# Attention scores as half-height matmuls on two halves of the array rows, and second-MoE slots of 288 rows

## The chip, the core and the metric

One core of a Trainium2 chip runs the whole program in one launch. The metric is the device time of one execution in microseconds (us). TensorE (PE, with its weight loads shown apart as PEld), VectorE (DVE), ScalarE (ACT), GpSimd (POOL) and the DMA queues work side by side and wait for each other through semaphores.

## The reference, cut to what matters

```python
# attention: 4 batches, 8 heads, 576 tokens, head size 64
scores = q @ k.T / 8
scores = where(scores >= max(scores) - tau, scores, -1e9)
x = softmax(scores) @ v                  # then heads joined: 2304 x 512
# first MoE: 512 -> 2048 -> 512
x = square(relu(x @ w_in)) @ w_out
# second MoE: 8 experts, 512 -> 1024 -> 512, each token to one expert
e = argmax(x @ w_gate)
out = gate_w * eom * (relu(x @ w1[e]) @ w2[e])
```

## The kernel before

All large products are float32r matmuls in three terms: each operand is split into a part that the array takes exactly (`[.., 0, ..]`, made on ACT) and the rest (`[.., 1, ..]`, made on DVE), and high*high, high*low and low*high are added in PSUM. A planner (`Graph.schedule`) sets the order of every engine's instructions from estimated durations and keys; the order is then fixed, and each engine works through its own list.

**Attention** (from 6 us to about 430 us). Two heads share a pair (16 pairs); a pair's q and k lie with one head in partitions 0 to 63 and the other in 64 to 127. A chunk (`t_chunk`, 144 of them) is 128 queries against 576 keys: scores (L636), row maximum on DVE (L639), exponential on ACT (L642), threshold on POOL, mask and sum on DVE (L651), scaling on POOL (L662), five transposes on PE (L705), copies on ACT (L713); `t_av` multiplies with v (L733) in matmuls that fill 64 array columns each, two side by side. The contraction of one head is only 64 long. So `t_op` builds, for each head, a 128-row operand by SBUF-to-SBUF DMA (`opA`, `opB`): k's high part above its low part, and q turned to match. Two 128-row steps then give all four products. Each step is two matmuls of 288 keys (`hf`), so a chunk has 4 matmuls. Eight of nine steps in `STEPS` are such chunks; the ninth (`hd == 2`) takes the last 64 queries of both heads with a block-diagonal q (`xd`) in three 128-row steps, 6 matmuls. The first four chunks (`EARLY`, L672) read q and k in place, in 64 array rows: the first two in rows 0 to 63, the next two in rows 64 to 127.

**First MoE.** The hidden layer (`t_h`, L843, matmuls of 288 columns) is woven into the attention as soon as a batch is done; the output layer follows (`t_y`, L1004, 256 columns). After each 256 tokens `t_gate` picks the experts.

**Second MoE** (from 687 us). Tokens of an expert are gathered by an indirect DMA into slots (`t_slot`): 256 rows ("p", `U == 2`: 96 matmuls of 256 columns, L1301, then 48 of 512, L1351) or 128 rows ("s": 24 of 512, L1321, and 24 of 512, L1351). Every slot loads its expert's two weight matrices. Two slots of 256 are filled early; `t_table` on DVE computes from the counts which expert the other 7 and 4 slots hold (`S2`, `S1`). More slots would run in a branch (`extra`). The counts of this input are 110, 394, 153, 77, 281, 410, 499 and 380 tokens; the 13 slots hold them without the branch.

Of the kernel before, what the change touches and what calls it, by code (L numbers as in the profile page):

```python
# [261 lines left out]
def moa(ctx, tc, q, k, v, tau, w_in, w_out, wg, wog, w1, w2, ctab, coln, out):  # L262
# [35 lines left out]
    W1, W2 = 55, 8.0  # L298
# [6 lines left out]
    W4 = 30  # L305
    W6 = 197
    W7 = 130
# [3 lines left out]
    S2 = 7  # L311
    S1 = 4
    NL2, NL1 = 12, 8
# [16 lines left out]
        "scores": (-6, -3),  # L330
        "max": (-17, 14),
        "exp": (17, 2),
        "bound": (-27, -12),
        "mask": (-19, -32),
        "sum": (-16, -6),
        "norm": (-19, 35),
        "turn": (8, 11),
        "parts": (8, 9),
        "av": (4, -17),
        "prep": (-2, 13),  # L340
        "x": (8, 22),
# [15 lines left out]
    MEMF, MEMR = 10608, 25728  # L357
# [78 lines left out]
    for nm, n, shape in (  # L436
        ("xk", 2, [P, 2, S]), ("xq", 1, [P, 2, S]), ("xd", 1, [P, 2, P]),
        ("opA", 2, [P, OPN]), ("opB", 2, [P, OPN]),
    ):
        at = mk(nm, at, n, shape, F32R)  # L440
# [9 lines left out]
    at = mk("gs", at, 2, [P, 256], F32, 2)  # L450
# [4 lines left out]
    at = mk("lt", at, 3, [P, 2, 2], I32, 2)  # L455
    at = mk("cs", at, 3, [P, 2], F32, 2)
    at = mk("tb", at, 1, [P, 576], F32, 2)
    at = max(at, DEC)
# [5 lines left out]
    mk("xg", at, 1, [P, 2, DM + 1], F32, 3)  # L464
# [3 lines left out]
    at = mk("raw", at, 1, [P, 2, 512], F32, 3)  # L468
    mk("wgb", 0, 1, [P, NKC, 32], F32R, 2)
# [5 lines left out]
    at = mk("w", ATT, 4, [P, 2, 512], F32R, 2)  # L475
    at = mk("x2", at, 2, [P, 2, NKC, 256], F32R, 2)
    mk("w", at, 1, [P, 2, 512], F32R, 2)
    mk("hT", OPS, 2, [P, 2, DFE // P, 256], F32R, 3)
# [17 lines left out]
    tabn = const.tile([P, 3], I32, name="tabn")  # L496
# [86 lines left out]
    def t_op(pr, j, key):  # L583

        xk, xq = xks[pr], xqs[pr]
        buf = opb[pr, j] = new("opB" if j else "opA", f"{pr}")
        rows = slice(64 * j, 64 * j + 64)
        q3 = lambda r: buf.t[r, S:].rearrange("p (x n) -> p x n", x=2).bitcast(F32)

        def put_k(x):  # L590
            nc.sync.dma_start(buf.t[64 * x : 64 * x + 64, :S].bitcast(F32), xk.t[rows, x].bitcast(F32))

        def put_q():
            nc.sync.dma_start(q3(slice(0, 64)), xq.t[rows, :, 64:].bitcast(F32))

        def turn_q(x):
            nc.sync.dma_start(q3(slice(64, 128))[:, 1 - x], xq.t[rows, x, 64:].bitcast(F32))

        parts = lambda xy, *xs: [t for x in xs for t in (q_tags(pr, x) if xy is xq else [(xy, x)])]
        for x in range(2):  # L600
            dma(lambda x=x: put_k(x), 64 * S * 4, parts(xk, x), [(buf, "k", x)], key)
        dma(put_q, 64 * 1024 * 4, parts(xq, 0, 1), [(buf, "q")], key)
        for x in range(2):
            dma(lambda x=x: turn_q(x), 64 * 512 * 4, parts(xq, x), [(buf, "t", x)], key)
# [10 lines left out]
    def t_chunk(n, key):  # L615
# [6 lines left out]
        halves = [slice(hf * HALF, (hf + 1) * HALF) for hf in range(2)]  # L622
        q0 = QOFF[c]
        xk = xks[pr]

        def mm():
            if hd == 2:

                xd = xds[pr].t
                ops = [(xd[:, x], xk.t[:, y]) for x, y in ((0, 0), (0, 1), (1, 0))]  # L630
            else:
                o = opb[pr, hd].t
                ops = [(o[:, S + i * 512 + q0 : S + i * 512 + q0 + P], o[:, :S]) for i in range(2)]
            for i, (qo, ko) in enumerate(ops):
                for hf in range(2):
                    nc.tensor.matmul(s.t[:, hf, :HALF], qo, ko[:, halves[hf]], start=(i == 0), stop=(i == len(ops) - 1))  # L636
# [27 lines left out]
        if n < EARLY:  # L664
            xq = xqs[pr]
            hr = slice(64 * hd, 64 * hd + 64)

            def mm():
                i = 0
                for qx, kx in ((0, 0), (0, 1), (1, 0), (1, 1)):  # L670
                    for hf in range(2):
                        nc.tensor.matmul(  # L672
                            s.t[:, hf, :HALF], xq.t[hr, qx, 64 + q0 : 64 + q0 + P], xk.t[hr, kx, halves[hf]],
                            start=(i == 0), stop=(i == 3),
                        )
                    i += 1

            rd = [(xk, x) for x in range(2)] + [(xq, x, 0) for x in range(2)]
            g.add("PE", c_pe(HALF) * 8, mm, rd, [s], key)
        elif hd == 2:  # L680
            rd = [(xk, x) for x in range(2)] + [(xds[pr], j) for j in range(2)]
            g.add("PE", c_pe(HALF) * 6, mm, rd, [s], key + K("scores", pr))
        else:
            o = opb[pr, hd]
            rd = [(o, "q")] + [(o, w, x) for w in "kt" for x in range(2)]
            g.add("PE", c_pe(HALF) * 4, mm, rd, [s], key + K("scores", pr))
# [270 lines left out]
    turn = {"op": []}  # L957
# [87 lines left out]
    def t_gate(v, key):  # L1045
        row = rows[v]
        x2 = Buf(ALL["x2"], f"yT{v}")
# [18 lines left out]
        def mm():  # L1066
            for kc in range(NKC):
                for x in range(2):
                    nc.tensor.matmul(lt.t[:32], wgb.t[:, kc], x2.t[:, x, kc],
# [77 lines left out]
    def t_transpose(src, i, x2, tag, key, rd, G=g, pool=ALL):  # L1147
# [4 lines left out]
        def tp():  # L1152
            for kc in range(NKC):
                nc.tensor.transpose(ps.t[:, kc * P : (kc + 1) * P], src.t[:, i, kc * P : (kc + 1) * P], ident)

        dst = lambda x: x2.t[:, x, :, i * P : (i + 1) * P]
        p3 = lambda: ps.t.rearrange("p (c n) -> p c n", c=NKC)
        grp("PE", 0.45, tp, rd, [ps], key)
        grp("ACT", c_act(512, True), lambda: nc.scalar.activation(dst(0), p3(), AF.Copy), [ps], [(x2, 0, i)], key)
        grp("DVE", c_dve(512), lambda: nc.vector.tensor_tensor(dst(1), p3(), dst(0).bitcast(F32), op=ALU.subtract),  # L1160
# [4 lines left out]
    def t_table(early, key):  # L1165

        tt, ts, stt = nc.vector.tensor_tensor, nc.vector.tensor_scalar, nc.vector.scalar_tensor_tensor
        def run():
# [3 lines left out]
            Q = view(tb.t[:, 72:88], [P, 2, 8], F32)  # L1172
            sq = view(tb.t[:, 96:160], [P, 8, 8], F32)

            def cum(n):
                tt(sq, n.rearrange("p (o e) -> p o e", o=1).broadcast_to([P, 8, 8]), ct("le", [P, 8, 8]), op=ALU.mult)
# [21 lines left out]
            if early:  # L1198
                nc.vector.tensor_copy(t, cnt)
                ts(full, t, 8, None, op0=ALU.arith_shift_right)  # L1200
                cum(full)
# [5 lines left out]
            ts(t, cnt, 127.0, None, op0=ALU.add)  # L1207
            ts(t, t, 7, None, op0=ALU.arith_shift_right)
            stt(t, d, -2.0, t, op0=ALU.mult, op1=ALU.add)
            ts(a, t, 1, None, op0=ALU.arith_shift_right)  # L1210
# [11 lines left out]

            ts(tmp[:, 0:1], tabn[:, 0:1], float(S2), None, op0=ALU.subtract)
            stt(tabn[:, 2:3], tabn[:, 1:2], float(S1), tmp[:, 0:1], op0=ALU.subtract, op1=ALU.max)
# [3 lines left out]
        grp("DVE", (2.73 if early else 5.89), run, [(c2, "base"), (c2, "tab")], [tb, "tabe" if early else "tabl"], key)  # L1228
# [3 lines left out]
    def t_slot(G, pool, tag, tab, s, U, rows_known, deps, key):  # L1232

        add = G.add
        n = U * P
# [4 lines left out]
        lt, xg, cs, x2, hT = (Buf(pool[x], f"{x}{tag}") for x in ("lt", "xg", "cs", "x2", "hT"))  # L1240
# [5 lines left out]
        def r_s():  # L1246
            regs["s"] = nc.sync.value_load(tab[0:1, s, 0:1], min_val=0, max_val=NLIST - 256)

        def f_list():
            nc.sync.dma_start(lt.t[:, :U], lst[bass.ds(regs["s"], n)].rearrange("(u p) t -> p u t", p=P))  # L1250
# [5 lines left out]
        for u in range(U):  # L1256
            add("POOL", 1.05,
                lambda u=u: nc.gpsimd.indirect_dma_start(
                    out=xg.t[:, u], out_offset=None, in_=y_scr[0:rows_known],
                    in_offset=bass.IndirectOffsetOnAxis(lt.t[:, u, 0:1].bitcast(U32), 0)),  # L1260
# [24 lines left out]
        for u in range(U):  # L1285
            t_transpose(xg, u, x2, f"x{tag}", key - 8, [(xg, u)], G, pool)
# [3 lines left out]
            [(xg, u) for u in range(U)] + [(x2, 0, u) for u in range(U)], [cs], key)  # L1290
        xr = [(x2, x, u) for x in range(2) for u in range(U)]
        combos = ((0, 0), (0, 1), (1, 0))
        if U == 2:
            for fc in range(8):
                ps = Buf(pool["ph"], f"h{tag}_{fc}")

                def mm(fc=fc, ps=ps):
                    i = 0
                    for a, x in ((0, 0), (1, 0), (0, 1)):
                        for kc in range(NKC):  # L1300
                            nc.tensor.matmul(ps.t[:, :256], w1b[kc][fc // 4].t[:, a, (fc % 4) * P : (fc % 4 + 1) * P],  # L1301
                                             x2.t[:, x, kc], start=(i == 0), stop=(i == 11))
                            i += 1

                add("PE", 12 * c_pe(256), mm, xr + [(w1b[kc][fc // 4], a) for kc in range(NKC) for a in range(2)], [ps],
                    key + 1.45 * fc)
                add("ACT", c_act(256, True),
                    lambda fc=fc, ps=ps: nc.scalar.activation(hT.t[:, 0, fc], ps.t[:, :256], AF.Relu),
                    [ps], [(hT, 0, fc)], key + 1.45 * fc)
                add("DVE", c_dve(256),  # L1310
                    lambda fc=fc, ps=ps: nc.vector.scalar_tensor_tensor(  # L1311
                        hT.t[:, 1, fc], ps.t[:, :256], 0.0, hT.t[:, 0, fc].bitcast(F32), op0=ALU.max, op1=ALU.subtract),
                    [ps, (hT, 0, fc)], [(hT, 1, fc)], key + 1.45 * fc)
        else:
            for h in range(2):
# [8 lines left out]
                for kc in range(NKC):  # L1324
                    add("PE", 3 * c_pe(512), lambda kc=kc, mm=mm: mm(kc), xr + [(w1b[kc][h], 0), (w1b[kc][h], 1)], [ps],
                        key + 2.6 * h + 0.65 * kc)
# [17 lines left out]
        k2 = key + (10.5 if U == 2 else 6.0)  # L1344
        for u in range(U):
# [8 lines left out]
            for fc in range(8):  # L1354
# [6 lines left out]
                [ps, cs], [ob], k2 + 5.2 * u + 5.2)  # L1361
# [7 lines left out]
    def pair_prep(pr, key):  # L1369
# [4 lines left out]
        for j in range(2):  # L1374
# [133 lines left out]
```

## Time and profile before

| what | value |
|---|---|
| median of 3 runs | 967.85 us (965.61 to 968.86) |
| the profiled execution | 965.47 us, span 963.7 us |
| PE busy | 932.3 us, 97% of the span |
| DVE, ACT, POOL busy | 716.4, 645.6, 361.3 us |
| granted TensorE clock | 0.998 |

PE's busy time includes the modelled tail of each matmul, so a pause shorter than that tail doesn't show as idle. The pace of a stream is read from the starts of rows that follow each other, not from the mean duration of one instruction.

### The profile page before, as it was taken

Reading aid. Unit: us, or ns where it says so; the run is one execution under the profiler, and the core shown is the slowest. Engines: PE = TensorE matmul, PEld = TensorE weight load, DVE = VectorE, ACT = ScalarE, POOL = GpSimd, SP = SyncE. Lnnn points to the kernel's source line nnn. Section 1 sums busy time; section 2 is a strip of 40 time slices with the busy share of each in tenths; the row PEclk is TensorE's granted clock in tenths of the full one; section 3 lists DMA queues with packets and bytes.
Section 4 is the critical chain, followed back from the end, with each engine's and each line's share of the span. In section 5 each row is a group of like instructions: output and inputs, shape, how many; then the busy total and the mean of one; then the engine's idle time right before and its main releaser. Section 6 shows DMA issues by size and latency. Waiting matters only on the chain. (4 is left out here: it accounts for less than half of the span.)

```text
span 963.7 us, 20604 instructions
## 1 busy us (share of the span) xinstructions
PE 932.3 (97%) x6842; PEld 846.0 (88%) x6842; DVE 716.4 (74%) x1635; ACT 645.6 (67%) x1431; POOL 361.3 (37%) x607
## 2 busy tenths in 40 slices
PE   7899999999999999999999999999898999999996
PEld 6667889889889889989999999999887989889895
DVE  6898988877777777788558767898778677777720
ACT  5898888878678777787554444444648676876731
POOL 4556778875656766642101000010113111211300
PEclk9999999999999999999999999999999999999999
DMA  6785797767778766478455888566959867977700
GB/s 176 181 221 141 204 253 201 213 166 212 234 214 231 228 198 201 158 226 246 136 143 133 190 185 194 134 171 140 260 170 338 307 229 262 309 248 257 264 23 25
DMA packets 162565, 193.25 MB, mean 201 GB/s; under 512 B 23567, under 2 KB 113167, under 8 KB 162450
## 3 DMA queue, kind: packets, MB, share of 16 engines
q1 hardware_dynamic: 158210, 181.33, 65.2%
q0 software_dynamic: 4096, 10.52, 3.5%
q8 instruction: 56, 0.92, 0.4%
q14 instruction: 59, 0.48, 0.2%
q10 hardware_dynamic: 144, 0.00, 0.0%
HBM read 122.39 MB, written 43.20 MB: 172 GB/s over the span
## 5 line engine op out<-in xcount | busy, mean ns | idle before, releaser
L651 DVE SCALAR_TENSOR_TENSOR memf<-banks,memf 128x576 f32<-128x576 f32 x144 | 116.3, 814 | 43.4 <-ACT memf L642 27.0
L843 PE MATMUL banks<-memr,w 128*128 128x288 f32 x960 | 145.0, 299 | 1.3 <-DVE memr L740 1.3
L843 PEld LDWEIGHTS banks<-memr,w 128*128 128x128 f32 x960 | 130.9, 188 | 5.3 <-issue 3.8
L1004 PE MATMUL banks<-w,memr 128*128 128x256 f32 x864 | 126.9, 284 | 0.0
L713 ACT ACTIVATE pt<-banks 128x384 f32<-128x384 f32 (+2 forms) x320 | 114.2, 419 | 14.0 <-PE banks L705 13.5
L642 ACT ACTIVATE memf<-banks,memf 128x576 f32<-128x576 f32 x144 | 107.1, 753 | 20.1 <-DVE memf L639 13.6
L984 ACT ACTIVATE memr<-memf 128x512 fp32r<-128x512 f32 x126 | 77.7, 631 | 63.3 <-PE banks L1004 57.4
L639 DVE TENSOR_REDUCE memf<-banks 128x1 f32<-128x576 f32 x144 | 107.5, 750 | 16.3 <-PE banks L636 14.6
L662 POOL TENSOR_SCALAR memf<-memf 128x576 f32<-128x576 f32 x136 | 112.9, 832 | 13.0 <-DVE memf L659 7.0
L636 PE MATMUL banks<-memr 128*128 128x288 f32 x592 | 108.8, 308 | 5.3 <-DVE memf L651 3.4
L1004 PEld LDWEIGHTS banks<-w,memr 128*128 128x128 f32 x864 | 112.3, 190 | 0.3
L705 PE MATMUL banks<-ident,memf 128*128 128x128 f32 x720 | 104.6, 274 | 6.3 <-ACT pt L713 4.2
L1004 PE MATMUL banks<-memr 128*128 128x256 f32 x648 | 99.6, 285 | 0.0
L705 PEld LDWEIGHTS banks<-ident,memf 128*128 128x128 f32 x720 | 84.2, 140 | 14.6 <-POOL memf L647 4.7
L880 POOL TENSOR_TENSOR memf<-memf 128x288 f32<-128x288 f32 x88 | 71.5, 822 | 66.4 <-DVE memf L880 37.0
L636 PEld LDWEIGHTS banks<-memr 128*128 128x128 f32 x592 | 83.8, 188 | 13.8 <-DVE memf L651 7.1
L1301 PE MATMUL banks<-memr,w 128*128 128x256 f32 x504 | 91.4, 283 | 0.9 <-DVE memr L1311 0.9
L1140 POOL DMA_INDIRECT lst<-memf x18 | 18.7, 1039 | 193.6 <-DVE memf L1132 108.8
L988 DVE TENSOR_TENSOR memr<-memf,memr 128x512 fp32r<-128x512 f32 x126 | 82.9, 695 | 10.5 <-ACT memr L984 10.5
L843 PE MATMUL banks<-memr 128*128 128x288 f32 x576 | 87.9, 299 | 0.9 <-ACT memf L849 0.9
L1004 PEld LDWEIGHTS banks<-memr 128*128 128x128 f32 x648 | 87.1, 190 | 0.0
L733 PE MATMUL banks<-pt,memf 128*64 128x256 f32 (+1 forms) x640 | 85.0, 411 | 1.2 <-DVE memf L651 0.9
(153 smaller groups left out, 1778.4 us busy)
## 6 DMA issues: line engine op xcount, KB each, us to landing
memf<-in_moe_w_dram SPq DMA_DIRECT2D x104, 512.0 KB
r_scr<-memf SPq DMA_DIRECT2D x192, 144.0 KB
memf<-r_scr SPq DMA_DIRECT2D x51, 512.0 KB
memr<-memr SPq DMA_DIRECT2D x64, 144.0 KB
memr<-memr SPq DMA_DIRECT2D x64, 128.0 KB
memr<-memr SPq DMA_DIRECT2D x32, 256.0 KB
memf<-in_moe_w_in_dram SPq DMA_DIRECT2D x32, 256.0 KB
memf<-in_moe_w_out_dram SPq DMA_DIRECT2D x32, 256.0 KB
```

The source lines that it names most:

```text
L636: nc.tensor.matmul(s.t[:, hf, :HALF], qo, ko[:, halves[hf]], start=(i == 0), stop=(i == len(ops) - 1))
L639: nc.vector.tensor_reduce(nm.t, s.t[:, :, :HALF], axis=AX.XY, op=ALU.max, negate=True)
L642: nc.scalar.activation(p.t[:, :S].rearrange("p (a n) -> p a n", a=2), s.t[:, :, :HALF], AF.Exp, bias=nm.t)
L651: nc.vector.scalar_tensor_tensor(p3, s.t[:, :, :HALF], th.t, p3, op0=ALU.is_ge, op1=ALU.mult, accum_out=sm.t)
L662: nc.gpsimd.tensor_scalar(p.t[:, :S], p.t[:, :S], sm.t, 1.0, op0=ALU.mult, op1=ALU.mult)
L705: nc.tensor.transpose(ps.t[:, i - a], p.t[:, i * P : (i + 1) * P], ident)
L713: lambda pt=pt, ps=ps, j=j, a=a, z=z, c0=c0, w=w, off=off: nc.scalar.activation(pt.t[:, j, a:z, off : off + w], ps.t[:, :, c0 : c0 + w], A ...
L733: nc.tensor.matmul(out(slice(64 * j, 64 * j + 64)), raw.t[:, j, c], pt.t[:, j, c, :N], start=(c == 0), stop=(c == NQ - 1))
L843: nc.tensor.matmul(ps.t[:, :HALF], wv[:, a, kc], xT.t[:, x, kc, half], start=(i == 0), stop=(i == len(seq) - 1),)
L988: lambda d=d, sq=sq: nc.vector.tensor_tensor(d(1), sq(), d(0).bitcast(F32), op=ALU.subtract),
L1004: nc.tensor.matmul(ps.t[:, :QT], o.t[:, a, f], w.t[:, x, cc], start=(f == 0 and i == 0), stop=(f == 7 and i == 2))
L1301: nc.tensor.matmul(ps.t[:, :256], w1b[kc][fc // 4].t[:, a, (fc % 4) * P : (fc % 4 + 1) * P], x2.t[:, x, kc], start=(i == 0), stop=(i == 11))
```

## The change

Scores: `t_op` now makes one tile for both heads (`ox`), in which each head's k and q lie in the other head's partitions; 4 DMAs a pair instead of 10. A chunk multiplies high*high, high*low and low*high in three steps (the fourth product is left out). In each step the first 288 keys are multiplied in array rows 0 to 63 and the other 288 in rows 64 to 127, as two 64-row matmuls into two PSUM banks: 6 matmuls a chunk. The `hd == 2` chunks stay as they are. The first four chunks also drop the fourth product (24 matmuls for 32).

Second MoE: an expert whose rest over a multiple of 128 is at most 32 gets a slot "W" of 256 + 32 rows. Its first layer is 96 matmuls of 288 columns; its second keeps w2 in place and streams the hidden rows (96 matmuls of 288, L1391), and its result is transposed back (L1405). With the counts above, 2 early p, 4 p, 4 s and 2 W slots run instead of 2 early p, 7 p and 4 s. The table on DVE grows (72 instructions for 49), and the early slots go to the largest experts. Buffers change places, and the planner's keys are new.

```diff
+        for j in range(2):
+            dma(lambda j=j: put_k(j), 64 * S * 4, ...)
+            dma(lambda j=j: put_q(j), 64 * 1024 * 4, ...)
...
-                o = opb[pr, hd].t
-                ops = [(o[:, S + i * 512 + q0 : S + i * 512 + q0 + P], o[:, :S]) for i in range(2)]
+            for i, (x, y) in enumerate(((0, 0), (0, 1), (1, 0))):
                 for hf in range(2):
+                    r = ROWS[hf]
+                    if hd == 2:
+                        qo, ko = xds[pr].t[:, x], xk.t[:, y, halves[hf]]
+                    elif hf == hd:
+                        qo, ko = xq.t[r, x, 64 + q0 : 64 + q0 + P], xk.t[r, y, halves[hf]]
+                    else:
+                        o = opb[pr].t
+                        qo, ko = o[r, S + x * 512 + q0 : S + x * 512 + q0 + P], o[r, y * HALF : (y + 1) * HALF]
+                    nc.tensor.matmul(s.t[:, hf, :HALF], qo, ko, start=(i == 0), stop=(i == 2))
...
-            g.add("PE", c_pe(HALF) * 4, mm, rd, [s], key + K("scores", pr))
+            g.add("PE", c_pe(HALF) * 3 + 0.02, mm, rd, [s], key + K("scores", pr))
...
-    S2 = 7
+    S2 = 4
+    SW = 2
+    ORDER = "psWspsWspp"
...
+            for c in range(NKC):
+                def mm(lo, hi, c=c, ps=ps):
+                    for f in range(lo, hi):
+                        for i, (a, x) in enumerate(combos):
+                            nc.tensor.matmul(ps.t[:, :N], w2b[f].t[:, x, c * P : (c + 1) * P], hT.t[:, a, f, :N],
+                                             start=(f == 0 and i == 0), stop=(f == 7 and i == 2))
+                        nc.tensor.transpose(ps.t[:n, c * P : (c + 1) * P], yT.t[:, c, u * P : u * P + n], ident)
```

The order on PE in the attention, where the hidden layer of the first MoE is woven in (before: L636 scores, L705 transposes, L733 product with v, L843 hidden layer):

```order
L733 MATMUL banks<-pt_83,memf 64x256 x10
L636 MATMUL banks<-memr 128x288 x8
L705 MATMUL banks<-ident,memf 128x128 x5
L843 MATMUL banks<-memr 128x288 x8
L705 MATMUL banks<-ident,memf 128x128 x5
L843 MATMUL banks<-memr 128x288 x8
L705 MATMUL banks<-ident,memf 128x128 x5
L843 MATMUL banks<-memr 128x288 x4
L636 MATMUL banks<-memr 128x288 x4
```

And of the change at a like place (L643, L708, L736 and L846 are the same four):

```order
L736 MATMUL banks<-pt_83,memf 64x256 x10
L643 MATMUL banks<-memr 128x288 x6
L708 MATMUL banks<-ident,memf 128x128 x5
L846 MATMUL banks<-memr 128x288 x8
L643 MATMUL banks<-memr 128x288 x6
L708 MATMUL banks<-ident,memf 128x128 x5
L846 MATMUL banks<-memr 128x288 x8
L708 MATMUL banks<-ident,memf 128x128 x3
L643 MATMUL banks<-memr 128x288 x6
```

A burst of 4 full-height score matmuls has become a burst of 6 half-height ones, and it still stands alone between full-height work. Counted over the whole order behind the first hidden-layer matmul: 91 chunks with half-height scores stand in 90 bursts; 82 bursts begin behind full-height work and 8 behind a product with v, and 82 end before full-height work, 44 of them before L846 and 38 before transposes. Ahead of it there are 33 such chunks (and the first four), in 25 bursts.

The order on PE near the end of a W slot of the change (L1391 its second layer, L1157 and L1371 transposes of slots, L1359 the first layer of the s slot behind it, L1405 the transposes of its result):

```order
L1391 MATMUL banks<-memr,w_71 128x288 x3
L1391 MATMUL banks<-memr,w_76 128x288 x3
L1359 MATMUL banks<-memr 128x512 x3
L1359 MATMUL banks<-w_73,memr 128x512 x3
L1405 MATMUL banks<-ident,memf 128x128 x8
L1359 MATMUL banks<-w_5614,memr 128x512 x3
L1405 MATMUL banks<-ident,memf 32x128 x4
L1359 MATMUL banks<-memr 128x512 x6
```

What was the second layer of a p slot (48 matmuls of 512 columns) is 96 of 288 in a W slot, with 12 transposes behind it among the next slot's first layer.

## Rows read from the trace of the kernel before

**Rows 1.** The page: busy time of each engine.

```profile
PE 932.3 (97%) x6842; PEld 846.0 (88%) x6842; DVE 716.4 (74%) x1635; ACT 645.6 (67%) x1431; POOL 361.3 (37%) x607
```

**Rows 2.** Stages: length; busy PE, PEld, DVE, ACT, POOL; clock, DMA share, GB/s.

```profile
0.00:92.30 92.30, 79.47 (x559) 61.09 (x560) 76.82 (x190) 71.89 (x157) 49.88 (x127) 1.00 0.69 180
92.30:485.50 393.20, 388.87 (x2984) 353.39 (x2983) 304.49 (x675) 306.14 (x744) 242.70 (x417) 1.00 0.71 207
...
686.80:742.30 55.50, 50.12 (x323) 44.06 (x322) 46.06 (x125) 34.90 (x76) 9.12 (x9) 1.00 0.77 255
742.30:955.90 213.60, 212.52 (x1297) 188.42 (x1295) 135.96 (x235) 135.72 (x271) 37.29 (x33) 1.00 0.65 223
```

**Rows 3.** Timeline of PE from 327 us: start, length, instructions merged.

```profile
327.13 0.69 PE L636 MATMUL banks<-memr 128*128 128x288 f32 x4
327.74 2.38 PE L733 MATMUL banks<-pt,memf 128*64 128x256 f32 x20
330.05 0.76 PE L705 MATMUL banks<-ident,memf 128*128 128x128 f32 x5
330.57 1.83 PE L843 MATMUL banks<-memr 128*128 128x288 f32 x12
332.24 0.70 PE L636 MATMUL banks<-memr 128*128 128x288 f32 x4
332.77 0.71 PE L705 MATMUL banks<-ident,memf 128*128 128x128 f32 x5
...
333.85 1.76 PE L843 MATMUL banks<-memr 128*128 128x288 f32 x12
335.45 0.71 PE L705 MATMUL banks<-ident,memf 128*128 128x128 f32 x5
```

**Rows 4.** Timeline of PE: products with v, a window from 328.45 us and one from 153.6 us.

```profile
328.23 1.90 PE L733 MATMUL banks<-pt,memf 128*64 128x256 f32 x16
...
153.88 2.38 PE L733 MATMUL banks<-pt,memf 128*64 128x256 f32 x20
156.19 0.80 PE L636 MATMUL banks<-memr 128*128 128x288 f32 x4
156.82 0.71 PE L705 MATMUL banks<-ident,memf 128*128 128x128 f32 x5
```

**Rows 5.** Timeline of PE around the gate's matmuls of 32 columns and of 32 rows.

```profile
510.21 1.08 PE L1069 MATMUL banks<-memr 128*32 128x256 f32 x8
511.13 0.52 PE L1004 MATMUL banks<-memr 128*128 128x256 f32 x3
511.49 0.52 PE L1004 MATMUL banks<-w,memr 128*128 128x256 f32 x3
511.94 0.30 PE L1078 MATMUL banks<-ident,memf 32*128 32x32 f32 x2
512.17 0.62 PE L1004 MATMUL banks<-w,memr 128*128 128x256 f32 x3
512.63 0.53 PE L1004 MATMUL banks<-memr 128*128 128x256 f32 x3
```

**Rows 6.** First weight load in 64 rows; then PE in two windows of 0.42 us.

```profile
6.25 0.28 PEld L672 LDWEIGHTS banks<-memr 64*128 64x128 f32 x1 [0.23 <-issue]
...
7.97:8.39 0.42, 0.42 (x6) 1.00 0.85 197
8.50:8.92 0.42, 0.42 (x9) 1.00 0.81 196
```

**Rows 7.** Timeline of PE in the second MoE: output layer of a p slot.

```profile
776.93 2.23 PE L1351 MATMUL banks<-w,memr 128*128 128x512 f32 x9
779.00 1.52 PE L1351 MATMUL banks<-memr 128*128 128x512 f32 x6
```

**Rows 8.** Timeline of DVE at the late table: its first and last of 33 instructions.

```profile
704.18 0.16 DVE L1196 TENSOR_TENSOR memf<-memf 128x8 f32<-128x8 f32 x1
...
710.23 0.18 DVE L1193 TENSOR_TENSOR tab<-memf 128x16 int32<-128x16 f32 x1
```

More of the change, by code (lines that the diff above doesn't have):

```diff
@@ L329, in moa @@
     PLACE = {
-        "scores": (-6, -3),
-        "max": (-17, 14),
+        "scores": (-4, -3),
+        "max": (-14, 14),
         "exp": (17, 2),
[L333 to L336, printed above, removed]
+        "bound": (-30, -12),
+        "mask": (-5, -32),
+        "sum": (-11, -7),
+        "norm": (-19, 41),
         "turn": (8, 11),
[L338 to L341, printed above, removed]
+        "parts": (8, 14),
+        "av": (8, -17),
+        "prep": (-2, 15),
+        "x": (8, 23),
     }
@@ L956, in moa @@
     rows = {}
-    turn = {"op": []}
+    turn = {"op": [], "slot": 0}
     def t_y(v, key):
@@ L1046, in t_gate @@
         row = rows[v]
-        x2 = Buf(ALL["x2"], f"yT{v}")
+        x2 = Buf(ALL["xB" if v % 2 == 0 else "xA"], f"yT{v}")
         for i in range(2):
@@ L1221, in run, with t_slot @@
             nc.vector.tensor_copy(tabn[:, 1:2], inc[:, 7:8])
-            ts(tmp[:, 0:1], tabn[:, 0:1], float(S2), None, op0=ALU.subtract)
-            stt(tabn[:, 2:3], tabn[:, 1:2], float(S1), tmp[:, 0:1], op0=ALU.subtract, op1=ALU.max)
             stt(Q[:, 0], cnt, 256.0, ct("ebd"), op0=ALU.mult, op1=ALU.add)
             slots(NL1, tab1, False)
-        grp("DVE", (2.73 if early else 5.89), run, [(c2, "base"), (c2, "tab")], [tb, "tabe" if early else "tabl"], key)
+            cum(wn)
+            nc.vector.tensor_copy(tabn[:, 2:3], inc[:, 7:8])
+            stt(Q[:, 0], od, 128.0, Q[:, 0], op0=ALU.mult, op1=ALU.add)
+            slots(NLW, tabw, False)
+            ts(tmp[:, 0:1], tabn[:, 0:1], float(S2), None, op0=ALU.subtract)
+            stt(tmp[:, 0:1], tabn[:, 1:2], float(S1), tmp[:, 0:1], op0=ALU.subtract, op1=ALU.max)
+            stt(tabn[:, 3:4], tabn[:, 2:3], float(SW), tmp[:, 0:1], op0=ALU.subtract, op1=ALU.max)
+        grp("DVE", (3.1 if early else 8.4), run, [(c2, "base"), (c2, "tab")], [tb, "tabe" if early else "tabl"], key)
     last = []
-    def t_slot(G, pool, tag, tab, s, U, rows_known, deps, key):
+    def t_slot(G, pool, tag, tab, s, U, rows_known, deps, key, R=0):
         add = G.add
-        n = U * P
+        UR = U + (R > 0)
+        N = U * P + R
+        rows = lambda u: P if u < U else R
         def dma(fn, nbytes, r, w, key, q="SP"):
             add(q, max(0.66, nbytes / 340e3), fn, r, w, key, lat=c_dma(nbytes) - max(0.66, nbytes / 340e3))
-        lt, xg, cs, x2, hT = (Buf(pool[x], f"{x}{tag}") for x in ("lt", "xg", "cs", "x2", "hT"))
+        side = "A" if G is not g else "AB"[turn["slot"] % 2]
+        turn["slot"] += 1
+        lt, xg, cs, x2, hT = (Buf(pool[x], f"{x}{tag}") for x in ("lt", "xg", "cs", "x" + side, "h" + side))
         regs = {}
@@ L1284, in t_slot @@
                     [raw, (w, 0)], [(w, 1)], kj)
-        for u in range(U):
-            t_transpose(xg, u, x2, f"x{tag}", key - 8, [(xg, u)], G, pool)
+        for u in range(UR):
+            t_transpose(xg, u, x2, f"x{tag}", key - 8, [(xg, u)], G, pool, rows(u))
         add("ACT", c_act(2),
@@ L1289, in t_slot @@
                 cs.t[:, :U].rearrange("p (u o) -> p u o", o=1), xg.t[:, :U, DM : DM + 1], AF.Copy),
-            [(xg, u) for u in range(U)] + [(x2, 0, u) for u in range(U)], [cs], key)
-        xr = [(x2, x, u) for x in range(2) for u in range(U)]
+            [(xg, u) for u in range(U)] + [(x2, 0, u) for u in range(U)], [(cs, 0)], key)
+        if R:
+            add("ACT", c_act(1),
+                lambda: nc.scalar.activation(cs.t[:R, U : U + 1], xg.t[:R, U, DM : DM + 1], AF.Copy),
+                [(xg, U), (x2, 0, U)], [(cs, 1)], key)
+        xr = [(x2, x, u) for x in range(2) for u in range(UR)]
         combos = ((0, 0), (0, 1), (1, 0))
@@ L1373, in pair_prep @@
             t_qk(pr, nm, key)
-        for j in range(2):
-            t_op(pr, j, key)
+        t_op(pr, key)
         t_diag(pr, key)
```

223 lines of the change are left out of this document (130 added, 93 removed).

## The prediction

> **What bounds the kernel now.** The page comes first: PE is busy 97% of the span and DVE, next, 74% [rows 1]. A share over the whole span can hide stages, so the stages come next [rows 2]. From 92.3 to 485.5 us, where scores, transposes, products with v and the first MoE's hidden layer are woven together, PE idles 4.3 us of 393.2; in the late slots of the second MoE 1.1 us of 213.6. There a microsecond of PE work is a microsecond of the span. Ahead of 92.3 us, with attention alone, PE idles 12.8 us and waits mostly for what DVE, ACT and POOL do with a chunk, so less PE work there gives little and more costs little. So I price the change in PE time, stage by stage, and in the third view, the timeline, look at what a matmul occupies. Starts that follow each other give the pace: four score matmuls start 0.53 us ahead of the next row, twelve of the hidden layer 1.60 us, which is 0.133 us for 288 columns either way [rows 3]; three of 256 columns take 0.36 us, 0.12 each [rows 5]; nine of 512 take 2.07 us, 0.23 each [rows 7].
>
> **Scores: what is removed.** A chunk had four steps of 0.133 us. Now it has three, if the two halves of a step run at once. That shows in the four early chunks, which already use 64 rows. In the window at 7.97 us, with only rows 0 to 63 at work, 6 matmuls are touched in 0.42 us; in the window at 8.50 us, where the chunks in rows 64 to 127 have begun, 9 [rows 6]. Two of each are the stragglers at the edges, which leaves about 4 against 7: two streams side by side, each at its own 0.13 us. I take the halves as fully parallel. Behind 92.3 us there are 91 such chunks: 91 x 0.133 = 12.1 us less.
>
> **Scores: what is added.** Each burst of half-height matmuls stands between full-height work. What does PE pay for going into another division of the array and back? The trace has three such places.
> The products with v use 64 columns. The four score matmuls ahead of one start 0.61 us before it, not 0.53: 0.08 us to get in. From its start to the next row are 2.31 us, while its ten pairs need 2.17 (sixteen instructions, eight pairs, take 1.90, the last of them 0.38 long, so 0.217 a pair): 0.14 us. Then five transposes take 0.52 us instead of 0.47: 0.05 more [rows 3, 4]. Together 0.27 us. Where score matmuls follow, four take 0.63 instead of 0.53 us [rows 4]: 0.32 to 0.33.
> The gate's back-transposes use 32 rows. Three matmuls at 511.49 would end at 511.85; the two small ones start at 511.94; the full-height ones behind them start at 512.17 and need 0.46 us for three instead of 0.36 [rows 5]. From 511.85 to 512.63 are 0.78 us, 0.42 more than three matmuls, with the two small ones in it.
> The first 64-row load waited 0.23 us for nothing that the profile shows, behind full-height matmuls [rows 6].
> Against it: the gate's eight matmuls of 32 columns run at 0.115 us and the next row follows without a gap [rows 5]. Those keep all 128 rows and one column place, so I count them as no change of division.
> A burst of scores is nearest to the v product: same length, same two edges. Its first weights are 128 columns wide, not 64, so the load that nothing covers is longer; behind a change such a load costs 0.10 us (the 0.63 for 0.53), where the v product's costs some 0.05 (its first two pairs take 2.38 - 1.90 = 0.48, not 0.43 [rows 4]). I add 0.06, a little more than the difference, since two loads stand there: 0.33 us before transposes, 0.39 before hidden-layer matmuls. Behind 92.3 us 38 bursts end before transposes and 44 before the hidden layer: 38 x 0.33 + 44 x 0.39 = 29.7 us. The 8 that touch a v product share its edges and cost nothing more. Bounds: 0.27 and 0.33 as measured (24.8 us), 0.42 for each (34.4 us). I take 29.7.
> Net for the scores there: 29.7 - 12.1 = **+17.6 us** (+12.7 to +22.3).
> The Trainium skill says in "TensorEngine Tiling (Array Packing)", section Tiling Modes, that changing the tiling mode, unlike changing the tile within a mode, drains TensorE. Rows 3 to 5 agree for 64 columns and 32 rows, and rows 6 agree that going from one row half to the other costs nothing; the 32-column matmuls don't show it. By the same page's speedup of up to 2x alone, without the drain, this term would be -12.1 us.
>
> **What else moves in the attention.** A slower PE leaves the others more time, so some of PE's 4.3 idle us in that stage [rows 2] go: -2.5 (0 to -4). Ahead of 92.3 us 33 chunks save 4.4 us and 22 bursts cost about 7.3, where PE idles 12.8 us anyway; the first four chunks drop 8 matmuls, at most 1.0 us: +0.5 (-1 to +3). The SBUF copies go from 10 to 4 a pair, 160 to 64 in all, on SP's queue; PE waits for none of them behind 92.3 us, and the DMA engines are at 0.71 of their time there [rows 2]: 0.
>
> **Second MoE.** A p slot is 96 x 0.12 + 48 x 0.23 + 8 transposes of about 0.1 (0.47 for five [rows 3]) = 23.3 us; an s slot 48 x 0.23 + 12 x 0.1 = 12.2. Seven and four make 211.9, against a stage of 213.6 with 1.1 idle [rows 2], so the prices hold. A W slot is 192 matmuls of 288 columns at 0.133 = 25.5, 24 transposes (16 full, 8 small) 2.1, and one or two changes of division for the 32 rows, 0.5: 28.1 us. Three p go and two W come: 56.2 - 69.9 = **-13.7 us** (-13 to -14.4 while PE is the bound). One slot less to load is 4.2 MB less, and DVE and ACT are busy 136 of 213.6 us [rows 2], so nothing else takes over.
> The late table has about 20 more small DVE instructions; 33 took 6.2 us [rows 8], some 0.18 each: 3.6 us on a DVE that is busy 46 of the 55.5 us of the early slots. Queued behind it are the hidden rows of an early slot and the next weights, for which PE waits; PE idles 5.4 us there already [rows 2]. +1.5 (0 to +3.6).
>
> **Sum.** 17.6 - 2.5 + 0.5 - 13.7 + 1.5 = +3.4 us. The profiled execution took 965.47 us, 2.4 below the median of 967.85; the sum is a difference, so I set it on the median: **971 us**. With all bounds on one side it is -5.7 or +15.9.
>
> **Rivals.**
> *No price for a change into 64 rows.* Only the 32-row and 64-column forms are measured in both directions; the 0.23 us of rows 6 is a single load near the start. Then the scores give -12.1, the early part -1, the second MoE -13.7 with the table's +1.5: -25, or 942 us. For it: the float32r matmuls of 32 columns pass without a gap. Against it: rows 5 show the price on a row division, both ways. 0.15.
> *The price is paid, but hidden more than I think.* The planner counts a burst as 0.42 us, PE needs 0.40 + 0.33 or more; results come in time for a late PE, so the waits vanish, and at 0.27 to 0.33 a burst the sum is 12.7 - 4 - 1 - 13.7 + 0.5 = -5.5: 962 us. 0.16.
> *A dearer change.* At 0.42 us for each of 82 bursts, nothing absorbed, the sum is 22.3 + 3 - 13.7 + 3.6 = +15: 983 us. With my other terms the sum is 82 times the price of a burst less 26.3: even at 0.32, slower by over 0.3% from 0.36. 0.06.
> *The halves run one after the other.* Then the change doesn't do what it says: six times 0.133 is 0.27 more than before, 91 x 0.27 = 24 in place of -12.1, about 1007 us. Rows 6 speak against it. 0.02.
> My own case, 965 to 978 us, has 0.61.
>
> **How the numbers follow.** 0.3% is 2.9 us, about what a measurement of this kernel can tell from no change. Slower means above 970.8: of my case a little more than half, 0.34, and the last two rivals, 0.08: 0.42. Faster means below 965: the first two rivals, 0.31, and 0.01 of my own. The rest, 0.26, is no change. The range 955 to 982 holds my case, most of the second rival and half of the third, about 0.8; the first rival stays outside.
>
> **What the profile after would show.** Score matmuls start in pairs a few ns apart, three pairs 0.13 us apart. If I am right, the first weight load of nearly every burst carries a wait put down to nothing, the row behind it is 0.05 to 0.1 us longer than its like, and the stage that ends with the first MoE's hidden layer grows from 485.5 to about 501 us, while the late slots shrink from 213.6 to about 200 us. If hidden-layer matmuls follow scores at 0.13 us, the first rival holds and the stage ends near 473. A late-slot stage that doesn't shrink by over 10 us would make the second part wrong: PE would then wait there for weights or DVE.

## The result, and the profile after

The changed kernel took 972.36 us (median of 15 executions, 969.47 to 976.14) beside 967.85 us for the kernel before (15 executions, 964.87 to 970.71): a ratio of 1.0052, 95% interval 1.0038 to 1.0066, or 5.0 us more by the ratio (the two medians lie 4.5 us apart). The kernel before was measured again beside each group of experiments, with medians from 964.3 to 967.9 us, so differences between kernels are worked out from the ratios to it unless the text says otherwise. The profiled execution of the change took 972.46 us, its span is 970.7 us; the one before had 963.7. So the two profiles lie 7.0 us apart, 2.5 more than the medians, because the profiled execution before was a good one of its kind.

First the page and the stages of the changed kernel, as in [rows 1, 2] (length; busy PE, PEld, DVE, ACT, POOL; clock, DMA share, GB/s). The last two rows are the early slots and the late slots of the second MoE; the cut is the first matmul of the first late p slot.

```profile
PE 939.0 (97%) x7058; PEld 826.9 (85%) x7058; DVE 702.6 (72%) x1634; ACT 633.2 (65%) x1416; POOL 361.8 (37%) x607
...
0.00:91.50 91.50, 81.32 (x614) 58.21 (x614) 78.59 (x190) 71.82 (x158) 49.34 (x127) 0.94 0.54 145
91.50:496.70 405.20, 404.71 (x3171) 344.11 (x3170) 299.89 (x674) 305.22 (x745) 244.69 (x417) 1.00 0.59 176
697.40:758.50 61.10, 53.30 (x323) 46.53 (x322) 50.04 (x145) 35.02 (x75) 10.25 (x9) 0.94 0.71 243
758.50:962.70 204.20, 198.93 (x1273) 179.56 (x1271) 120.88 (x210) 124.36 (x255) 34.94 (x33) 1.00 0.63 207
```

Against [rows 2], the stage of scores and hidden layer grew by 12.0 us (393.2 to 405.2), and PE idles 0.5 us in it instead of 4.3. The early slots grew by 5.6 us (55.5 to 61.1), at a granted clock of 0.94. The late slots shrank by 9.4 us (213.6 to 204.2): PE works 13.6 us less there (198.93 for 212.52), but idles 5.3 us instead of 1.1.

The timeline of PE in the changed kernel at a place like [rows 3]:

```profile
331.12 0.66 PE L643 MATMUL banks<-memr 64*128 64x288 f32 x6
331.71 0.80 PE L846 MATMUL banks<-memr,w 128*128 128x288 f32 x4
332.36 0.71 PE L708 MATMUL banks<-ident,memf 128*128 128x128 f32 x5
...
337.50 1.82 PE L846 MATMUL banks<-memr 128*128 128x288 f32 x12
339.25 0.66 PE L643 MATMUL banks<-memr 64*128 64x288 f32 x6
339.84 0.77 PE L708 MATMUL banks<-ident,memf 128*128 128x128 f32 x5
340.36 0.91 PE L846 MATMUL banks<-memr 128*128 128x288 f32 x5
```

Read the starts around the burst at 339.25. Twelve hidden-layer matmuls behind transposes handed over after 1.67 us before (330.57 to 332.24 in [rows 3]); the burst starts after 1.75. Six half-height matmuls, three pairs side by side, need 0.40 us; the next row starts 0.59 behind them. The five transposes take 0.52, not 0.47. That is 0.08 + 0.19 + 0.05 = 0.32 us around a burst that ends before transposes, where the prediction has 0.33. The halves do run at once: one after the other, six matmuls would have needed 0.80.

What PE waited for in the second MoE of the changed kernel (line, releaser: us in total, times, longest; PEq is PE's own sequencer):

```profile
PE banks L1157 <- DMA memf<-y_scr,memf: 4.3, 3, 2.5
PE banks L1371 <- ACT memf L1365: 3.4, 2, 1.7
PE banks L1425 <- PEq L1529: 1.8, 1, 1.8
PE banks L1157 <- DVE memf L1017: 1.8, 1, 1.8
PE banks L1425 <- DVE memr L1349: 1.3, 1, 1.3
```

The second row is new, and its cause stands on ACT. The timeline of ACT in the changed kernel at one of its two places, and behind the "..." the row of PE that waits:

```profile
829.44 0.68 ACT L1410 ACTIVATE memf<-banks,memf 32x512 f32<-32x512 f32 x1 [2.03 <-DMA out_dram<-memf]
830.03 0.61 ACT L1312 ACTIVATE w<-memf 128x512 fp32r<-128x512 f32 x1
830.55 0.57 ACT L1365 ACTIVATE memf<-banks 128x512 f32<-128x512 f32 x1
...
831.17 0.66 PE L1371 MATMUL banks<-ident,memf 128*128 128x128 f32 x4 [1.65 <-ACT memf L1365]
```

L1410 writes the third output block of a W slot, the one of 32 rows. There are two output buffers (`ob`), and the DMA that empties the older one has not landed: ACT stands 2.03 us. The relu of the s slot behind it (L1365) is queued on ACT, and PE's transposes (L1371) wait for that.

### The profile page after: what moved, and what is told of

It reads as the page before. It is cut to its first block, busy times and chain, and to the rows that moved or that the text cites. A ratio compares the mean times of both kernels' runs of the same rounds, so it can differ in the third digit from the quotient of the medians.

```text
span 970.7 us, 20783 instructions
## 1 busy us (share of the span) xinstructions
PE 939.0 (97%) x7058; PEld 826.9 (85%) x7058; DVE 702.6 (72%) x1634; ACT 633.2 (65%) x1416; POOL 361.8 (37%) x607
## 4 chain that ended last, share of the span: by engine, by line
PE 79%; DMA 8%; issue 4%; DVE 4%; ACT 3%; POOL 1%; POOLq 0%; SPq 0%; ACTq 0%; DVEq 0%
PE banks L846 21%; PE banks L1007 17%; PE banks L736 8%; PE banks L708 8%; PE banks L643 8%; PE banks L1338 6%; PE banks L1425 5%; DMA memf<-y_scr,memf 3%; DMA memf<-in_moe_w_dram 2%; PE banks L1391 2%; DMA out_dram<-memf 1%; PE banks L1157 1%; PE banks L1359 1%; ACT pt L716 1%; ACT memf L649 1%
## 5 line engine op out<-in xcount | busy, mean ns | idle before, releaser
L846 PE MATMUL banks<-memr,w 128*128 128x288 f32 x960 | 148.4, 302 | 0.0
L846 PEld LDWEIGHTS banks<-memr,w 128*128 128x128 f32 x960 | 130.3, 188 | 7.4 <-issue 5.8
L716 ACT ACTIVATE pt<-banks 128x384 f32<-128x384 f32 (+2 forms) x320 | 119.6, 415 | 16.7 <-PE banks L708 15.6
L1007 PE MATMUL banks<-w,memr 128*128 128x256 f32 x864 | 123.1, 284 | 0.0
L708 PE MATMUL banks<-ident,memf 128*128 128x128 f32 x720 | 111.2, 281 | 5.8 <-ACT pt L716 4.0
L708 PEld LDWEIGHTS banks<-ident,memf 128*128 128x128 f32 x720 | 82.6, 142 | 23.0 <-issue 11.0
L643 PE MATMUL banks<-memr 64*128 64x288 f32 (+1 forms) x840 | 98.9, 325 | 0.7 <-DVE memf L658 0.4
L1007 PE MATMUL banks<-memr 128*128 128x256 f32 x648 | 94.4, 284 | 0.0
L846 PE MATMUL banks<-memr 128*128 128x288 f32 x576 | 90.6, 303 | 0.5 <-ACT memf L852 0.5
L1315 DVE TENSOR_TENSOR w<-memf,w 128x512 fp32r<-128x512 f32 x110 | 72.0, 688 | 22.8 <-ACT w L1312 21.8
L643 PEld LDWEIGHTS banks<-memr 64*128 64x128 f32 (+1 forms) x840 | 68.4, 188 | 23.0 <-issue 12.7
L1338 PE MATMUL banks<-memr 128*128 128x256 f32 (+1 forms) x396 | 86.4, 288 | 0.4 <-DVE memr L1163 0.4
L736 PE MATMUL banks<-pt,memf 128*64 128x256 f32 (+1 forms) x640 | 84.7, 411 | 0.2
```

The source lines that it names most:

```text
L643: nc.tensor.matmul(s.t[:, hf, :HALF], qo, ko, start=(i == 0), stop=(i == 2))
L708: nc.tensor.transpose(ps.t[:, i - a], p.t[:, i * P : (i + 1) * P], ident)
L716: lambda pt=pt, ps=ps, j=j, a=a, z=z, c0=c0, w=w, off=off: nc.scalar.activation(pt.t[:, j, a:z, off : off + w], ps.t[:, :, c0 : c0 + w], A ...
L736: nc.tensor.matmul(out(slice(64 * j, 64 * j + 64)), raw.t[:, j, c], pt.t[:, j, c, :N], start=(c == 0), stop=(c == NQ - 1))
L846: nc.tensor.matmul(ps.t[:, :HALF], wv[:, a, kc], xT.t[:, x, kc, half], start=(i == 0), stop=(i == len(seq) - 1),)
L1007: nc.tensor.matmul(ps.t[:, :QT], o.t[:, a, f], w.t[:, x, cc], start=(f == 0 and i == 0), stop=(f == 7 and i == 2))
```

## The experiments

**Each part alone.** The first two kernels split the change; the diff is cut to the lines that tell. With the score part alone the second MoE stays as before (`S2 = 7`, no W slots); with the slots' part alone the scores stay as before.

```diff
 # scores alone, from the kernel before
...
-            g.add("PE", c_pe(HALF) * 4, mm, rd, [s], key + K("scores", pr))
+            g.add("PE", c_pe(HALF) * 3 + 0.02, mm, rd, [s], key + K("scores", pr))
...
 # slots alone, from the kernel before
-    S2 = 7
+    S2 = 4
+    SW = 2
...
+    ORDER = "psWspsWspp"
...
```

> The kernel before with the score part of the change alone (three steps on row halves, the copies and the order that go with them); second MoE as before. My theory (each change into 64 rows and out again costs 0.33 to 0.39 us, each step saves 0.133 us): +11 to +15 us against the kernel before, that is about 980 us, and the hidden layer's stage ends near 497 us. Rival, no price for 64 rows: -12 to -15 us, about 954 us, stage end near 473 us. Rival, the price is paid but hidden by other waits: within 3 us of before.

Measured: 975.75 us, ratio 1.0104 (1.0084 to 1.0124), +10.1 us, a little under what was expected.

> The kernel before with the second MoE's part of the change alone (W slots of 288 rows, the table and the order of slots that go with them); scores as before. My sum from the slots' PE time: -12 to -14 us, about 955 us. My theory after the result: the slots save that PE time, but waits for an output buffer, for a gather and two stretches at the lower clock give back 5 to 9 us, so -4 to -8 us, about 962 us. Rival, the slots' part is worth its whole sum and the loss comes from the new scores' order: -12 us or more.

Measured: 960.20 us, ratio 0.9939 (0.9916 to 0.9962), -5.9 us. The stages, of scores alone (scores and hidden layer):

```profile
91.60:497.70 406.10, 405.12 (x3172) 344.45 (x3171) 299.89 (x674) 305.59 (x745) 243.69 (x417) 1.00 0.58 176
```

and of slots alone (scores and hidden layer, then the second MoE):

```profile
94.70:488.60 393.90, 389.03 (x2985) 353.37 (x2984) 304.39 (x675) 304.84 (x744) 242.73 (x417) 1.00 0.70 206
689.10:950.80 261.70, 251.94 (x1594) 226.34 (x1592) 170.82 (x354) 159.56 (x329) 43.72 (x41) 0.99 0.64 218
```

The parts add up: 1.04% - 0.61% = 0.43% beside 0.52% for the whole change, a difference within the intervals. The score part makes its stage 12.9 us longer and leaves PE 1 us idle in it, so the loss is PE time, not a wait. The rival without a price wanted -12 to -15 us, the rival with a hidden price no more than 3; both are out. The slots give less than the -12 to -14 us of their PE work.

**The price by itself.** Two kernels add the same 124 matmuls of 32 columns to the changed kernel, one per half-height chunk. In one they stand ahead of the burst, among full-height work; in the other inside it, behind the first pair, so that PE leaves the half-height division and comes back once more.

```diff
 # ahead of the burst
+            if hd != 2:
+                nc.tensor.matmul(s.t[:, 0, :32], xk.t[:, 0, :P], xk.t[:, 0, :32], start=True, stop=True)
 # in the middle of it (inside the loop over the three steps)
+                if hd != 2 and i == 1:
+                    nc.tensor.matmul(s.t[:, 0, 320:352], xk.t[:, 0, :P], xk.t[:, 0, :32], start=False, stop=False)
```

> The changed kernel with one more matmul of 32 columns on all 128 rows put ahead of each of the half-height score bursts (its result is overwritten by the burst). It stands among full-height work, so it adds no change of division: my theory and the rival both give 122 x about 0.03 to 0.1 us, +3 to +12 us against the changed kernel. It is the control for the run in which the same matmul stands in the middle of the burst.

Measured: 975.36 us, ratio 1.0106 (1.0080 to 1.0131), 5.2 us over the changed kernel, as expected.

> The changed kernel with the same matmul of 32 columns on 128 rows put between the first and the second step of each half-height score burst (its result goes to columns that nothing reads), so that each burst is left and entered once more. My theory, a price of 0.3 to 0.4 us for each change out and in again: 30 to 45 us more than the run with that matmul ahead of the burst. Rival, the division changes for nothing and the time comes from the score part's order and waits: the same time as that run, within 4 us.

Measured: 1020.36 us, ratio 1.0568 (1.0538 to 1.0598). One burst in the timeline of the kernel with the matmul ahead:

```profile
402.52 0.28 PE L634 MATMUL banks<-memr 128*128 128x32 f32 x1
402.74 0.67 PE L645 MATMUL banks<-memr 64*128 64x288 f32 x6
403.34 0.76 PE L710 MATMUL banks<-ident,memf 128*128 128x128 f32 x5
```

and one of the kernel with it in the middle:

```profile
405.58 0.40 PE L645 MATMUL banks<-memr 64*128 64x288 f32 x2
405.91 0.28 PE L635 MATMUL banks<-memr 128*128 128x32 f32 x1
406.12 0.53 PE L645 MATMUL banks<-memr 64*128 64x288 f32 x4
406.58 0.77 PE L710 MATMUL banks<-ident,memf 128*128 128x128 f32 x5
```

From burst to transposes are 0.60 us in the first and 1.00 in the second, with the small matmul in it. By the medians of the two kernels, measured side by side, the same matmul costs 45.0 us more in the middle: 45.0 / 124 = **0.363 us for one change out and in again**. In the stage of scores and hidden layer alone it is (442.7 - 409.5) / 91 = 0.365:

```profile
106.20:548.90 442.70, 442.19 (x3262) 365.99 (x3261) 300.13 (x671) 306.97 (x743) 241.51 (x416) 1.00 0.53 161
```

(the kernel with it in the middle), and

```profile
94.50:504.00 409.50, 408.66 (x3262) 357.73 (x3261) 301.49 (x674) 305.54 (x745) 244.22 (x417) 1.00 0.58 175
```

(the one with it ahead).

The Trainium skill says in "TensorEngine Tiling (Array Packing)", section Tiling Modes, that a change of the tiling mode drains TensorE while tiles within a mode work independently. Both halves agree with the runs here: 0.36 us for the one, pairs side by side for the other. How much of the 0.36 us is such a drain, and how much the first weight load that nothing covers, no run tells apart.

**Fewer bursts.** If the price is one per burst, two chunks in one burst pay it once.

```diff
+            if first:
+                s2, q2 = Buf(pS, f"s{n + 1}"), QOFF[c + 1]
+                ahead[n + 1] = s2
+
+                def both():
+                    mm()
+                    mm(s2, q2)
+
+                g.add("PE", c_pe(HALF) * 6 + 0.02, both, rd, [s, s2], key + K("scores", pr))
```

> The changed kernel, with the scores of two neighbouring half-height chunks put into one burst of twelve matmuls from chunk 36 on (48 bursts fewer; both score buffers are taken at once). My theory, a price per burst of 0.33 to 0.39 us: 16 to 18 us less than the changed kernel, minus what the taken buffers cost in waits, so -8 to -18 us, 954 to 964 us. Rival, the loss lies in the single half-height matmuls or loads, or in the order: within 3 us of the changed kernel.

Measured: 962.10 us, ratio 0.9965 (0.9945 to 0.9985), 8.4 us under the changed kernel, at the near end of what was expected and outside the rival's 3 us. The timeline of PE has the paired burst, twelve matmuls in 0.99 us where 0.80 is their pace: the same 0.19 as six paid.

```profile
336.21 1.06 PE L647 MATMUL banks<-memr 64*128 64x288 f32 x12
337.20 1.86 PE L860 MATMUL banks<-memr 128*128 128x288 f32 x12
```

The stage has 47 bursts instead of 90, 43 x 0.365 = 15.7 us less to pay, but it is only 7.1 us shorter (398.1 for 405.2 us). PE's waits in it are back:

```profile
PE banks L722 <- ACT pt L730: 2.6, 4, 0.9
PE banks L860 <- ACT memf L866: 1.0, 1, 1.0
PE banks L860 <- DVE memr L757: 0.6, 1, 0.6
PE banks L860 <- POOL w L797: 0.5, 1, 0.5
```

By the starts of rows these waits come to 6.8 us, against 0.65 in the changed kernel. That gives back 6 of the 15.7; three more chunks fall into this stage and take another 1.2; some 1.3 us are left unexplained. A joint burst takes both score buffers at once; that this is what brings the waits was not tried apart.

**The waits of the second MoE.** A third output buffer, in the changed kernel and with the slots alone; then, on top, earlier due times for a slot's list and gathers.

```diff
+    at += 8
     LT = at
...
+    mk("ob", 4224, 1, [P, DM], F32, 3)
     at = mk("ob", 0, 2, [P, DM], F32, 3)
 # and for the earlier lists and gathers
-        dma(f_list, 2048, [("reg", tag, 0)] + deps, [lt], key - 24)
+        dma(f_list, 2048, [("reg", tag, 0)] + deps, [lt], key - 30)
-                [lt, "y0"] + [("ys", u) for u in range((rows_known - 1) // P)], [(xg, u)], key - 12, lat=6.5)
+                [lt, "y0"] + [("ys", u) for u in range((rows_known - 1) // P)], [(xg, u)], key - 20, lat=6.5)
```

> The changed kernel with three output buffers (pool ob) in place of two in the second MoE. My theory: the W slot's third output block no longer waits for a buffer, ScalarE's next relu isn't queued behind that wait, and PE's two waits for it (3.4 us together) go: -2 to -4 us against the changed kernel, about 969 us. Rival: the block waits for the scatter's queue anyway, or PE's time goes into the next wait: within 1 us of the changed kernel.

Measured: 968.26 us, ratio 1.0030 (1.0015 to 1.0045), 2.1 us under the changed kernel.

> The kernel with the second MoE's part alone (scores as before) and three output buffers. My theory: -2 to -3 us against the run with that part alone, as its waits for ScalarE behind the buffer (2.6 us) go: about 957.5 us, 9 us under the kernel before. Rival: within 1 us of the run with that part alone.

Measured: 958.88 us, ratio 0.9935 (0.9919 to 0.9952): 0.4 us under slots alone, which is no difference: the rival's case.

> The same with three output buffers, and lists and gathers of a slot given earlier due times (30 in place of 24, 20 in place of 12 ahead of the slot), so that gathers stand ahead of scatters on POOL. My theory: PE's waits for gathered rows (1.4 to 4.3 us in the runs so far, with or without a stretch at the lower clock behind them) shrink: -1 to -3 us against the run with three buffers alone, about 955.5 us. Rival: the gather waits for its buffer or for the list, not for its place in the queue: within 1 us.

Measured: 956.97 us, ratio 0.9916 (0.9892 to 0.9939), 1.9 us under the run with three buffers alone, with intervals that overlap.

> The changed kernel with three output buffers and the earlier due times of lists and gathers. Theory: -1 to -3 us against the changed kernel with three buffers alone (968.3), so 965 to 967, level with the kernel before: the price of the score bursts (+12 us) and the second MoE's whole gain (-11 to -12 us) then cancel. Rival: the gather's wait isn't decided by its place in the queue with these scores: within 1 us of 968.3.

Measured: 964.45 us, ratio 1.0003 (0.9985 to 1.0020), 4.7 us under the changed kernel and level with the kernel before.

PE's waits in the second MoE, slots alone with two buffers:

```profile
PE banks L1375 <- ACT memf L1369: 2.6, 2, 1.5
...
PE banks L1161 <- DMA memf<-y_scr,memf: 1.4, 2, 1.0
```

with three buffers, where the wait for ACT is gone and the one for gathered rows longer:

```profile
PE banks L1163 <- DMA memf<-y_scr,memf: 3.6, 2, 2.7
```

and with three buffers and the earlier gathers:

```profile
PE banks L1377 <- ACT memf L1371: 1.6, 1, 1.6
...
PE banks L1163 <- DMA memf<-y_scr,memf: 0.3, 1, 0.3
```

The wait for ACT in this last list is another one: no buffer holds ACT up, but a weight that has not landed, with the relu L1371 queued behind it.

```profile
769.81 0.63 ACT L1318 ACTIVATE w<-memf 128x512 fp32r<-128x512 f32 x1 [1.01 <-DMA memf<-in_moe_w_dram]
```

So each edit removes the wait at which it aims, and part of the time goes into the next. In the time, both edits together are clear in the changed kernel (1.0003 for 1.0052). The third buffer alone is likely there, as its interval and that of the changed kernel just overlap, and with the old scores neither step is clear of noise. In the changed kernel the gather at 741.78 us stood on POOL behind a scatter that had waited 6.07 us; before, the gather went ahead, at 725.14. Here POOL of the changed kernel:

```profile
740.02 1.45 POOL L1437 DMA_INDIRECT out_dram<-memf  x1 [6.07 <-DMA memf<-in_moe_w_dram]
741.78 1.22 POOL L1291 DMA_INDIRECT memf<-y_scr,memf  x1 [0.31 <-PE banks L1338]
```

and POOL of the kernel before:

```profile
725.14 1.49 POOL L1258 DMA_INDIRECT memf<-y_scr,memf  x1 [4.26 <-issue]
```

**The clock.** In the kernel with three buffers and earlier gathers PE waits at the start of the second MoE, and then the granted clock falls. Windows of that kernel:

```profile
688.80:693.70 4.90, 2.62 (x22) 2.18 (x21) 3.87 (x8) 2.95 (x6) 0.00 (x0) 1.00 0.98 320
693.70:697.70 4.00, 4.00 (x24) 4.00 (x23) 2.94 (x6) 3.58 (x7) 0.00 (x0) 0.57 0.82 280
```

The last kernel fills that wait with transposes of the identity.

```diff
+    FILL = {f"y{TILES // 2 - 1}1": 18, "xe00": 10, "xe01": 4}
...
+            for _ in range(FILL.get(f"{tag}{i}", 0)):
+                nc.tensor.transpose(ps.t[:, :P], ident, ident)
```

> The run with three buffers and earlier gathers, with 32 transposes of the identity (some 0.11 us each, their results overwritten) put ahead of the three transposes at the start of the second MoE for which PE waits 2 to 3 us (the last row tile's second half and the first gathered rows). Theory: the granted clock falls to 0.5 for some 4 us there because PE stood idle; with PE busy in the wait the fall goes, the mean clock of the runs rises by about 0.002 from 0.992, and the time falls by 0 to 2 us from 957 (the fillers take some of it back where rows come in time). Rival: the fall has nothing to do with that wait, or such transposes don't hold the clock: the fall stays in the profile, and the time is the same or 1 to 3 us more.

Measured: 953.97 us, ratio 0.9888 (0.9866 to 0.9909). Windows of it at the same place:

```profile
690.70:694.90 4.20, 4.20 (x41) 4.20 (x39) 3.58 (x8) 2.80 (x7) 0.00 (x0) 1.00 0.96 337
694.90:698.90 4.00, 4.00 (x36) 3.93 (x35) 3.68 (x7) 3.66 (x9) 0.00 (x0) 1.00 0.81 260
```

PE is busy through the wait, the clock stays at 1.00, and 36 matmuls are touched in 4 us where there were 24. The mean clock of six executions rose from 0.992 to 0.994. That the fillers hold the clock is likely and not shown: of the other eleven profiled kernels nine have a fall at the start of the second MoE, but two have none without fillers, the kernel before and the one with the matmul in the middle of the burst. The time fell by 2.7 us, but the two intervals overlap and the two profiled executions are level (956.67 and 956.75 us), so the gain is likely and not shown either. This kernel, the old scores with the new slots, a third buffer, earlier gathers and fillers, is the fastest of the study, 10.8 us under the kernel before.

## Why the prediction was right, point by point

The terms of the sum, and what the profiles and the experiments gave for each:

| term | forecast, us | found, us |
|---|---|---|
| scores: three steps for four, and the changes | -12.1 + 29.7 = +17.6 | -12.1 + 82 x 0.365 = +17.8 |
| waits absorbed in that stage | -2.5 | -4.9 |
| that stage in all | +15.1 | +12.0 (scores alone +12.9) |
| ahead of it | +0.5 | -0.8 |
| output layer of the first MoE | 0 | -0.5 |
| late slots, PE work | -13.7 | -13.6 |
| late slots, new waits | 0 | +4.2 |
| early slots (table, gathers, clock) | +1.5 | +5.6 |
| sum | +3.4 | +6.9 (spans of the profiles +7.0, medians +4.5, by the ratio +5.0) |

**The price** was the step on which the forecast hung, and it was sized right: 0.362 us a burst on average from the v products, 0.363 and 0.365 by experiment. The starts of rows over the whole stage, set against like places of the kernel before, say the same burst by burst: in the median 0.33 us for the 30 bursts that end before transposes and 0.39 for the 44 before hidden-layer matmuls, away from the products with v. At those the prediction was wrong both ways: the 8 bursts ahead of one cost 0.19 us each and not nothing, the 8 behind one about 0.15 and not 0.33, which cancels. So the rivals "no price" and "dearer change" fall by the size of the price, and "one after the other" by the timeline.

**The absorbed waits** were mis-sized. I took 2.5 of the 4.3 idle microseconds of [rows 2]; but idle time counts only from the modelled end of a matmul. By the starts, eight waits of the kernel before in that stage come to 5.6 us, and 0.65 are left after the change. One of them in the timeline of the kernel before:

```profile
197.65 0.79 PE L636 MATMUL banks<-memr 128*128 128x288 f32 x4
199.12 0.52 PE L705 MATMUL banks<-ident,memf 128*128 128x128 f32 x3 [0.67 <-POOL memf L656]
```

Four matmuls at 0.133 us end their turn at 198.18; the next starts at 199.12. PE lost up to 0.94 us there and the row shows 0.67. The rival "hidden more than I think" had this half right: nearly all waits went, but the pool was 5.6 us and not enough to hide the price. Of the 12.9 us that the two terms make, the profile shows 12.0; the rest is not explained.

**The second MoE** is where a step failed: "nothing else takes over". The PE work fell as priced, to 0.1 us. The other engines did have time on average, as the busy shares of [rows 2] say, but a W slot has three output blocks for two buffers, and the wait for one stood in ACT's queue ahead of a relu that PE needed: 3.4 of the 4.2 us. By the prediction's own sign, a late-slot stage that doesn't shrink by over 10 us, this part was wrong: it shrank by 9.4. Only the engine was another: PE waited for ACT, not for weights or DVE. The early slots cost 5.6 us instead of 1.5. The same 323 PE instructions were busy 3.2 us longer there (53.30 for 50.12), at a mean clock of 0.94, and PE idled 2.4 us more (7.8 for 5.4), which is about what the gather behind the scatter cost (2.49 us of waiting where the like wait before was 0.27). DVE worked 4.0 us more there (50.04 for 46.06), about the 3.6 us of the longer table, but no wait of PE names it.

Of the prediction's other signs most came: the half-height matmuls start in pairs 0 to 13 ns apart, the first weight load of each of the 90 bursts in that stage waits (0.165 us in the median, 55 times for nothing that the profile shows), and the stage ends at 496.7 us where about 501 was forecast.

The likeliest sign (slower) and the range hold, and the median lies 1.4 us from the forecast. That it lies so near is luck: there are two errors of opposite sign, 3.1 us too much in the stage of scores and hidden layer and 8.4 too little in the second MoE, and a reference execution 2.4 us under its median. One sum in the prediction is off: all its lower bounds together make -6.7 us, not -5.7 (the -1 of the part ahead of 92.3 us was left out); the range did not rest on it.

## What to carry to other kernels

Here half-height matmuls would pay only in longer bursts: a burst saved one step of 0.133 us a chunk and paid 0.36 for the change, so by this sum, which no run tried, it would have to hold three chunks to win. Two, with the waits that they brought, still left the stage 4.9 us over full-height scores (1.2 of them for three more chunks in it). When a slot gets one more output block, count the output buffers, and look at which instruction is queued on the copying engine behind the wait. And read waits from starts, not from idle time, where the ends of matmuls are modelled.

## What the runs showed of the hardware

The granted clock fell behind short waits. In the changed kernel two stretches in the second MoE have about half the clock, right behind PE's waits at 699 to 702 and 745 to 750 us:

```profile
702.00:706.00 4.00, 3.52 (x17) 3.52 (x18) 1.21 (x4) 1.11 (x3) 0.00 (x0) 0.57 1.03 414
750.00:754.00 4.00, 4.00 (x13) 3.14 (x12) 1.66 (x4) 2.66 (x6) 0.49 (x1) 0.57 0.35 107
```

In the second, six matmuls of 512 columns take 2.37 us from the first start (749.89) to the row behind them (752.26), where 0.23 us each would be 1.38; the granted clock goes to 1.2 from 2.4 GHz there. The Trainium skill, in "TensorE: Matmul & The Clock Gate", section What's actually happening, says that the gate follows how busy TensorE has been; the run with fillers agrees, with the clock at 1.00 where it was 0.57. But the kernel before waited at the like places too (0.27 and 1.46 us at 732 to 735) without a fall, and the run of scores alone, with its old slots, had one at 702 us: which wait brings one differs between executions and kernels.

It matters for the reading of small differences. The mean clock was 0.989 in the 15 executions of the change and 0.995 in the 53 of the kernel before that ran beside the experiments; and within the 15, the two at 0.995 took 971.04 and 969.47 us, those at 0.985 and 0.986 took 976.14 and 975.63. By that some 2 to 3 of the 5 us go with the clock, a correlation and not an experiment. Several kernels also show half the clock from about 10 to 20 us after the start (0.94 in the first window of the change), with no stage longer for it; what brings that was not tried.
